# Recurrent attention and a gated feed-forward on one core: eps as a 385th column, PSUM rings named tile by tile, and another order of all steps

## The chip, the core and the metric

The kernel runs on one core of a Trainium2 chip. Five engines work side by side, each through its own list of instructions in a fixed order: TensorE (PE in the profile, with its weight loads as PEld), VectorE (DVE), ScalarE (ACT), GpSimd (POOL) and SyncE (SP), which here only issues transfers. The metric is the device time of one run in microseconds (us).

## What is computed

The reference first runs a recurrence over 768 tokens for 4 batches x 8 heads of width 48, and then a feed-forward over the 3072 tokens of width 384:

```python
# attention, for each token t; state is 48x48 per batch and head
y[t]  = r[t] @ (state + (u*k[t])^T v[t])
state = w[t][:, None] * state + k[t]^T v[t]
# feed-forward on x = y, heads side by side
xn  = x / sqrt(mean(x*x) + 1e-6) * rms_g
g   = xn @ w_gate
out = (g * sigmoid(g) * (xn @ w_val)) @ w_out
```

Inputs and output are float32; the kernel multiplies in bfloat16 and sums in float32.

## The kernel before

The tokens are cut into 6 blocks of 128 for each of the 4 batches. A step is named `step.n.j`: n is the block, j the batch (or, in the feed-forward, the unit of work x). Blocks 0 and 1 of a batch are loaded together and treated as a pair of 256 tokens.

For each block the attention part does the following. `load_w`, `load_r`, `load_k`, `load_v` bring the inputs in (SP). `ln` takes the log of w (ACT), `cs_mm` (and `cs_k`, `cs_add`) makes its prefix sums by matmul (PE, DVE), `exp_r` and `exp_k` turn them into factors (ACT), `r_mul` and `k_mul` scale r and k with them (DVE; most k_mul on POOL). `rk_pe` transposes the result on PE and `rk_tr` copies it out (in blocks 0 and 1), or `rk_tr` is a transposing transfer. `q_mm` makes the 128x128 score tiles (even heads and odd heads apart), `q_mask_e`, `q_copy_o` and `q_mask_o` mask them into the tile `qts`, `st_mm` and `st_new` carry the state, `y_mm` makes the attention's output in PSUM. `bonus_mul`, `bonus_sum` and `bonus_v` make the u term (POOL, DVE, POOL), whose u was spread over the partitions once by `gu_mm` and `gu_out`. `x_add` adds both into `xb` (DVE). `x_sq` squares it on ACT and sums the row, `x_rstd` makes the reciprocal root, `xn_mul` applies it. `xn_pe` with `xn_out`, or the transfer `xn_tr` with `xn_gain` on POOL (blocks 4 and 5), lays the tile out for the feed-forward as `xnt`.

The feed-forward of a block of 512 tokens has 12 units x. `gate_mm.n.x` and `val_mm.n.x` are 3 matmuls of 512 columns each (in block 0, 6 of 256), `silu` (ACT) empties the gate's PSUM bank into `sg`, `h_mul` (DVE) multiplies the value's bank with it into `ht`. `o_mm` is 12 matmuls of 384 columns, `o_out` copies its bank out, `out_dma` stores it. The weights come by `load_gv` and `load_wo`, issued by POOL: the first gates need `load_gv.1.0` (wg_sb), the first values `load_gv.1.1` (wv_sb). `warm` is a matmul of zeros; 13 stand at the start, the rest fill places where PE would wait.

Nothing is scheduled by the compiler: the table ORDER is a list of 1096 steps, and each engine's list is the order in which its instructions are met there. Small sets say which engine a step uses: CAST_ACT, XN_DVE, RK_DVE, ODD_DVE, RSTD_ACT, OUT_DVE. PSUM's 8 banks are in three rings: "a" (2 banks: gates and prefix sums), "b" (2: values and the k sums), "q" (4: all else). A step that needs a bank takes the longest unused one of its ring whose last user stands earlier in ORDER, and waits on the chip until that user is done.

ACT holds one table of functions at a time. `act()` loads "ln and exp" or "silu" when the step needs the other one than the last step did (L236); Copy and Square need no change. `x_rstd` is Ln and Exp on ACT where RSTD_ACT says so, otherwise on POOL two operations, scale and eps (L589) and a power (L590).

## Time and profile before

| | |
|---|---|
| median of 3 runs | 199.46 us (199.08 to 203.08) |
| span of the profiled execution, first to last instruction | 197.62 us |
| median of the runs less that span | 1.84 us |
| PE busy | 191.5 us of the span, 97% |
| DVE, ACT, POOL busy | 156.4, 139.1, 127.5 us |
| granted TensorE clock | 1.000 |
| table loads on ACT | 14, 1283 ns each |
| moved by transfers | 32.42 MB, mean 164 GB/s |

The profile does not give the profiled execution's own device time beside its span; the runs' median stands next to it in the table. "L646" in a row is line 646 of the kernel, `ps_au` the first bank of ring "a" (u, v, x, z number the banks), `A<-B` says that a tile A is made from B, and `<-PE ps_av` behind an idle time names what ended it. A group row has busy us and the mean ns of one, and then the idle time ahead of it. Matmuls overlap, so the distance from start to start is what one costs.

### The profile page before, as it was taken

What the parts mean: (1) busy time and instruction counts of PE and PEld (TensorE: products, weight loads), DVE (VectorE), ACT (ScalarE), POOL (GpSimd) and SP (SyncE); (2) the same over time, 40 slices, a digit from 0 to 9 for tenths busy, and PEclk for the clock granted to TensorE, in tenths of its full rate; (3) what the DMA queues carried; (4) which work ended last, traced back from release to release, by engine and by line L of the source; (5) the groups of instructions that cost most, each with busy time, mean ns of one, the idle gap of its engine ahead of it and who ended that gap; (6) DMA issues with size and microseconds to landing.
All of it is one profiled execution on the core that took longest, in us unless ns stands there. A gap on an engine that the chain in (4) does not pass through costs nothing.

```text
span 197.6 us, 4751 instructions
## 1 busy us (share of the span) xinstructions
PE 191.5 (97%) x1742; PEld 120.4 (61%) x1742; DVE 156.4 (79%) x315; ACT 139.1 (70%) x286; POOL 127.5 (64%) x181
## 2 busy tenths in 40 slices
PE   7899999999999999999999999999999999999994
PEld 3456677888665556655655655666655655555563
DVE  5699998999997999989799988997689842435530
ACT  3989998979997889795699875698556760514201
POOL 3399999988599759793969998599661544000000
PEclk9999999999999999999999999999999999999999
DMA  6999999999897999999999967924580021012112
GB/s 164 320 325 267 244 220 205 220 213 197 174 230 162 199 179 214 200 211 214 185 206 225 202 147 166 227 51 145 134 216 12 5 60 60 20 63 80 40 60 101
DMA packets 109807, 32.42 MB, mean 164 GB/s; under 512 B 104276, under 2 KB 108632, under 8 KB 109784
## 3 DMA queue, kind: packets, MB, share of 16 engines
q1 hardware_dynamic: 107744, 28.58, 63.4%
q0 software_dynamic: 2032, 3.54, 10.0%
q8 instruction: 13, 0.21, 0.5%
q14 instruction: 10, 0.08, 0.1%
q10 hardware_dynamic: 8, 0.00, 0.0%
HBM read 25.96 MB, written 4.72 MB: 155 GB/s over the span
## 4 chain that ended last, share of the span: by engine, by line
PE 83%; DMA 7%; POOL 6%; SPq 1%; issue 1%; ACT 0%; POOLq 0%
PE ps_bu L646 13%; PE ps_bv L646 12%; PE ps_av L646 11%; PE ps_au L646 11%; PE ps_qv L683 7%; PE ps_qx L683 6%; PE ps_qz L683 6%; DMA wv_sb<-in_moe_w_val_dram 5%; PE ps_qu L683 5%; DMA kt<-in_k_dram 2%; POOL ruk L464 1%; POOL ruk L465 1%; SPq L248 1%; POOL qts L536 1%; PE ps_qz L513 1%
## 5 line engine op out<-in xcount | busy, mean ns | idle before, releaser
L238 ACT ACTIVATE sg<-ps_av 128x512 bf16<-128x512 f32 x36 | 21.5, 596 | 27.1 <-PE ps_av L646 21.4
L683 PEld LDWEIGHTS <-ht 128*128 128x128 bf16 x312 | 28.6, 98 | 18.3 <-DVE ht L666 0.4
L646 PEld LDWEIGHTS <-wg_sb 128*128 128x128 bf16 x252 | 27.0, 114 | 16.6 <-issue 0.3
L646 PEld LDWEIGHTS <-wv_sb 128*128 128x128 bf16 x252 | 26.4, 114 | 16.0 <-DMA wv_sb<-in_moe_w_val_dram 0.7
L666 DVE TENSOR_TENSOR ht<-ps_bu,sg 128x512 bf16<-128x512 f32 x37 | 25.4, 687 | 10.7 <-PE ps_bu L646 8.3
L666 DVE TENSOR_TENSOR ht<-ps_bv,sg 128x512 bf16<-128x512 f32 x35 | 24.0, 686 | 9.9 <-PE ps_bv L646 8.5
L646 PE MATMUL ps_bu<-xnt,wv_sb 128*128 128x512 bf16 (+1 forms) x135 | 30.3, 343 | 0.5 <-DMA wv_sb<-in_moe_w_val_dram 0.5
L646 PE MATMUL ps_av<-xnt,wg_sb 128*128 128x512 bf16 (+1 forms) x126 | 29.4, 350 | 0.0
L646 PE MATMUL ps_au<-xnt,wg_sb 128*128 128x512 bf16 (+1 forms) x126 | 29.3, 349 | 0.1
L646 PE MATMUL ps_bv<-xnt,wv_sb 128*128 128x512 bf16 (+1 forms) x117 | 28.5, 358 | 0.0
L464 POOL TENSOR_TENSOR ruk<-rt,kt 128x384 f32<-128x384 f32 x24 | 24.0, 1002 | 1.9 <-DVE diag L469 1.4
L465 POOL TENSOR_TENSOR ruk<-ruk,u_bc 128x384 f32<-128x384 f32 x24 | 24.0, 1000 | 1.9
L238 ACT ACTIVATE sg<-ps_au 128x512 bf16<-128x512 f32 x36 | 21.5, 596 | 4.5 <-PE ps_au L646 3.3
L457 POOL TENSOR_TENSOR rk<-kt,ek 128x384 bf16<-128x384 f32 x20 | 19.8, 1001 | 6.6 <-DMA kt<-in_k_dram 5.5
L475 POOL TENSOR_TENSOR ydiag<-vt,diag 128x384 f32<-128x384 f32 x24 | 19.9, 836 | 1.0 <-DVE diag L469 1.0
L236 ACT ACT_TABLE_LOAD x14 | 18.0, 1283 | 1.9 <-PEq L729 1.6
L536 POOL TENSOR_SCALAR_AFFINE_SELECT qts<-qts 128x512 bf16<-128x512 bf16 x19 | 11.9, 637 | 11.2 <-ACT qts L533 8.0
L683 PE MATMUL ps_qv<-wo_sb,ht 128*128 128x384 bf16 (+1 forms) x96 | 15.5, 311 | 0.0
L581 ACT ACTIVATE junk<-xb 128x384 bf16<-128x384 f32 x24 | 12.5, 521 | 4.2 <-DVE xb L576 3.9
L469 DVE TENSOR_REDUCE diag<-ruk 128x8 f32<-128x384 f32 x24 | 13.0, 544 | 0.0
L683 PE MATMUL ps_qx<-wo_sb,ht 128*128 128x384 bf16 x72 | 12.7, 326 | 0.0
L683 PE MATMUL ps_qz<-wo_sb,ht 128*128 128x384 bf16 x72 | 12.7, 326 | 0.0
(212 smaller groups left out, 376.8 us busy)
## 6 DMA issues: line engine op xcount, KB each, us to landing
out_dram<-ob SPq DMA_DIRECT2D x19, 192.0 KB, 2.4
wt<-in_w_dram SPq DMA_DIRECT2D x16, 192.0 KB, 4.2
rt<-in_r_dram SPq DMA_DIRECT2D x16, 192.0 KB, 4.4
vt<-in_v_dram SPq DMA_DIRECT2D x16, 192.0 KB, 3.7
kt<-in_k_dram SPq DMA_DIRECT2D x16, 192.0 KB, 4.0
wt<-in_w_dram SPq DMA_DIRECT2D x4, 384.0 KB, 4.3
rt<-in_r_dram SPq DMA_DIRECT2D x4, 384.0 KB, 4.9
kt<-in_k_dram SPq DMA_DIRECT2D x4, 384.0 KB, 4.9
```

Of the source, the lines that this page charges most:

```text
L236: nc.scalar.preload_act_table_set(table_name)
L238: return nc.scalar.activation(**kw).ins
L457: eng.tensor_tensor(out=rk[:, n % 2, j, 1, :, 0:D], in0=inp["k", n, j], in1=bank["cs_k", n, j][:, 0:DM].rearrange("p (h d) -> p h d", h=H) ...
L464: eng.tensor_tensor(out=ruk[n, j], in0=inp["r", n, j], in1=inp["k", n, j], op=ALU.mult)
L465: eng.tensor_tensor(out=ruk[n, j], in0=ruk[n, j], in1=u_bc, op=ALU.mult)
L469: nc.vector.tensor_reduce(out=diag[n, j].rearrange("p h o -> p (h o)"), in_=ruk[n, j], axis=mybir.AxisListType.X, op=ALU.add)
L475: eng.tensor_tensor(out=ydiag[n, j], in0=inp["v", n, j], in1=diag[n, j].to_broadcast([128, H, D]), op=ALU.mult)
L536: nc.gpsimd.affine_select(out=qts[n, j][:, 1], in_=qts[n, j][:, 1], compare_op=ALU.is_ge if n < 2 and j // 4 < n else ALU.is_gt, fill=0.0, ...
L581: nc.scalar.activation(out=junk, in_=xb[n, j], func=AF.Square, accum_out=rstd[n, j][:, 0:1])
L646: nc.tensor.matmul(ps.rearrange("p (i t) -> p i t", t=cols.stop - cols.start)[:, i, :], lhsT=units(ws, c, fs.start + i), rhs=xnt[n][:, c, ...
L666: nc.vector.tensor_tensor(out=ht[n][:, fs, cols], in0=bank.pop(("v", n, f)).rearrange("p (i t) -> p i t", i=fs.stop - fs.start), in1=bank. ...
L683: nc.tensor.matmul(ps[:, cols], lhsT=ht[n][:, f, b * L:(b + 1) * L], rhs=wo_sb[:, f, cols], start=(f == 0), stop=(f == FC - 1))
```

## The change

Three things, in one diff.

1. The sum of squares is finished on ACT. `xb` is no longer a rotating tile of 384 columns but one of 4 rows of `xrow`, with a 385th column that holds the square root of 384 eps. The Square has scale 384^-0.5 and runs over 385 columns, so its row sum is mean(x*x) + eps. On POOL only the power is left, and on ACT the Ln has no scale and no bias. The multiplication by rms_g in blocks 4 and 5 was on POOL and stays there; the unused other branch goes.
2. Tables MOVED_Q, MOVED_A and MOVED_B name a ring for 231 PSUM tiles; `psum()` looks there first. Gates and values may now lie in "q", scores, states and outputs in "a" or "b".
3. All of ORDER is new (1090 steps: 32 warm for 34, 15 q_mask_o for 19, else the same steps), and so are the sets. By the two programs: table loads 14 to 20; xn products on DVE 6 to 13; o_out on DVE 11 to 7; rk_tr copies on DVE 4 to 2; score tiles masked on DVE 45 to 49, copied by ACT 19 to 15; casts of v on ACT 13 to 14; Ln and Exp pairs on ACT 8 to 6; POOL's scale-and-eps operations 16 to none and its powers 16 to 18. SP issues the same 136 transfers.

```diff
-    CAST_ACT = sel("00 01 02 03 10 13 20 21 31 32 41 52 53")
+    CAST_ACT = sel("00 01 02 10 11 12 23 30 31 33 41 42 50 51")
-    XN_DVE = sel("02 21 23 42 43 51")
+    XN_DVE = sel("03 12 13 21 30 32 33 40 41 42 43 50 51")
-    RK_DVE = sel("00 11 12 13")
-    ODD_DVE = sel("00 01 02 04 12 13 15 16 20 21 43 50 53")
-    RSTD_ACT = sel("00 10 11 21 22 23 41 42")
-    OUT_DVE = sel("02 11 22 23 30 33 41 42 50 52 53 54")
+    RK_DVE = sel("00 02")
+    ODD_DVE = sel("04 06 07 10 11 12 13 15 16 22 23 32 40 42 43 50 52")
+    RSTD_ACT = sel("10 20 23 32 33 42")
+    OUT_DVE = sel("02 03 23 31 41 43 55")
...
     def psum(ring, key, shape, dtype=FP32):
+        ring = moved.get(key, ring)
         slots = rings[ring]
...
+    xrow = const.tile([128, NXB, DM + 16], FP32)
+    nc.vector.memset(xrow[:, :, DM:DM + 1], (eps * DM) ** 0.5)
...
     def x_add(n, j):
-        xb[n, j] = pt.tile([128, DM], FP32, name="xb", bufs=NXB)
-        nc.vector.tensor_tensor(out=xb[n, j], in0=bank.pop(("y", n, j)),
+        k = min((x for x in range(NXB) if xslots[x][0] < at[0]), key=lambda x: xslots[x])
+        xslots[k] = [xlast[n, j], NXB + at[0]]
+        xb[n, j] = xrow[:, k, 0:DM + 1]
+        nc.vector.tensor_tensor(out=xb[n, j][:, 0:DM], in0=bank.pop(("y", n, j)),
                                 in1=ydiag[n, j].rearrange("p h d -> p (h d)"), op=ALU.add)
     def x_sq(n, j):
-        nc.scalar.activation(out=junk, in_=xb[n, j], func=AF.Square, accum_out=rstd[n, j][:, 0:1])
+        nc.scalar.activation(out=junk[:, 0:DM + 1], in_=xb[n, j], func=AF.Square, scale=DM ** -0.5,
+                             accum_out=rstd[n, j][:, 0:1])
     def x_rstd(n, j):
-            act(LN_EXP, out=ss, in_=ss, func=AF.Ln, scale=1.0 / DM, bias=eps_col)
+            act(LN_EXP, out=ss, in_=ss, func=AF.Ln)
...
-            nc.gpsimd.tensor_scalar(out=ss, in0=ss, scalar1=1.0 / DM, scalar2=eps, op0=ALU.mult, op1=ALU.add)
             nc.gpsimd.tensor_tensor(out=rstd[n, j][:, 1:2], in0=ss, in1=mhalf, op=ALU.pow)
```

What the new order does is seen in the engines' lists, at the places that the prediction speaks of. First POOL, from the load of the first gate weights (wg_sb, `load_gv.1.0`) to that of the first value weights (wv_sb, `load_gv.1.1`); ydiag is bonus_v, the affine select q_mask_o, rk a k_mul, vb a cast of v; the numbers tell tiles of one name apart. Before:

```order
L350 DMA wg_sb4_138<-in_moe_w_gate_dram 128x3x1024
L475 TENSOR_TENSOR ydiag_346<-vt_278,diag_283 128x384
L536 AFFINE_SELECT qts_314<-qts_314 128x512
L536 AFFINE_SELECT qts_363<-qts_363 128x512
L475 TENSOR_TENSOR ydiag_440<-vt_278,diag_402 128x384
L536 AFFINE_SELECT qts_474<-qts_474 128x512
L384 CAST vb_500<-vt_348 128x384
L350 DMA wv_sb4_140<-in_moe_w_val_dram 128x3x1024
```

And now:

```order
L357 DMA wg_sb4_136<-in_moe_w_gate_dram 128x3x1024
L550 AFFINE_SELECT qts_285<-qts_285 128x512
L489 TENSOR_TENSOR ydiag_385<-vt_381,diag_383 128x384
L550 AFFINE_SELECT qts_326<-qts_326 128x512
L471 TENSOR_TENSOR rk_129<-kt_460,ek_416 128x8x48
L489 TENSOR_TENSOR ydiag_478<-vt_381,diag_308 128x384
L550 AFFINE_SELECT qts_474<-qts_474 128x512
L606 TENSOR_TENSOR rstd_513<-rstd_513,mhalf_126 128x1
L357 DMA wv_sb4_138<-in_moe_w_val_dram 128x3x1024
```

A k_mul and the power of the first block have come in between, and a cast has left.

Second DVE, up to its first h_mul (`ht`), which is the first reader of a value unit. Before, the score masks (`qts` with `up`) among its last rows are three:

```order
L451 TENSOR_TENSOR rk_131<-rt_400,ps_bv_423 128x8x48
L457 TENSOR_TENSOR rk_131<-kt_404,ps_qu_627 128x8x48
L576 TENSOR_TENSOR xb_728<-ps_qz_709,ydiag_704 128x384
L523 TENSOR_TENSOR qts_699<-ps_qx_689,up_117 128x512
L528 TENSOR_TENSOR qts_699<-ps_qv_690,up_117 128x512
L523 TENSOR_TENSOR qts_754<-ps_qu_744,up_117 128x512
L489 COPY rkT_775<-ps_qx_766 128x1024
L619 TENSOR_TENSOR xnt_633<-ps_qv_784,gT_77 128x3x128
L666 TENSOR_TENSOR ht_789<-ps_bu_777,sg_680 128x2x256
```

Now seven stand there, those of the q_mm that moved ahead of the first value unit on PE among them:

```order
L465 TENSOR_TENSOR rk_129<-rt_548,ps_qv_556 128x8x48
L537 TENSOR_TENSOR qts_672<-ps_qx_662,up_117 128x512
L537 TENSOR_TENSOR qts_749<-ps_qz_739,up_117 128x512
L542 TENSOR_TENSOR qts_760<-ps_au_751,up_117 128x512
L537 TENSOR_TENSOR qts_760<-ps_qu_750,up_117 128x512
L542 TENSOR_TENSOR qts_795<-ps_bv_786,up_117 128x512
L537 TENSOR_TENSOR qts_795<-ps_qz_785,up_117 128x512
L537 TENSOR_TENSOR qts_821<-ps_bu_811,up_117 128x512
L635 TENSOR_TENSOR xnt_591<-ps_bv_842,gT_77 128x3x128
L635 TENSOR_TENSOR xnt_591<-ps_qz_857,gT_77 128x3x128
L678 TENSOR_TENSOR ht_892<-ps_au_825,sg_720 128x2x256
```

The first value unit lies in a bank of ring "a" now (ps_au, before ps_bu), and more score tiles are masked ahead of it.

Third ACT in the feed-forward of block 3 (`sg` is a silu, `lw` an ln of a later block, `ob` an o_out, `vb` a cast). Before:

```order
L238 ACTIVATE ek<-ps_bv 128x384
L238 ACTIVATE lw<-wt 128x8x48 x2
L236 ACT_TABLE_LOAD
L238 ACTIVATE sg<-ps_av 128x512
L238 ACTIVATE sg<-ps_au 128x512
L692 COPY ob<-ps_qv 128x384
L238 ACTIVATE sg<-ps_av 128x512
```

Now:

```order
L247 ACTIVATE sg<-ps_qz 128x512
L394 CAST vb<-vt 128x384 x2
L245 ACT_TABLE_LOAD
L247 ACTIVATE lw<-wt 128x8x48
L245 ACT_TABLE_LOAD
L247 ACTIVATE sg<-ps_qx 128x512
L245 ACT_TABLE_LOAD
L247 ACTIVATE lw<-wt 128x8x48
L704 COPY ob<-ps_qz 128x384
L245 ACT_TABLE_LOAD
L247 ACTIVATE sg<-ps_qu 128x512
```

Two ln that stood together ahead of the silu units stand alone between them, with a table load on each side.

235 lines of the change are left out of this document (121 added, 114 removed).

## The prediction

> **What bounds the kernel now.** I read the busy shares first, then the table by stages, then TensorE (PE) in order of time, then who waits for whom.
>
> ```profile
> PE 191.5 (97%) x1742; PEld 120.4 (61%) x1742; DVE 156.4 (79%) x315; ACT 139.1 (70%) x286; POOL 127.5 (64%) x181
> ```
>
> The table by stages, with busy us (instructions) of PE, weight loads, DVE, ACT and POOL, then the granted clock:
>
> ```profile
> 0.00:10.80 10.80, 8.86 (x62) 5.00 (x63) 6.95 (x29) 6.26 (x10) 4.38 (x15) 1.00 0.91 249
> 10.80:25.80 15.00, 14.29 (x209) 8.86 (x207) 15.00 (x33) 14.87 (x33) 14.71 (x19) 1.00 1.16 276
> 25.80:30.80 5.00, 4.51 (x65) 3.74 (x65) 5.00 (x10) 4.95 (x10) 4.75 (x7) 1.00 1.11 209
> 30.80:75.00 44.20, 44.20 (x474) 32.17 (x475) 41.56 (x80) 38.71 (x75) 36.15 (x49) 1.00 1.01 197
> 75.00:130.00 55.00, 54.98 (x475) 32.61 (x474) 49.77 (x99) 43.44 (x96) 44.39 (x62) 1.00 0.94 196
> 130.00:160.00 30.00, 30.00 (x255) 17.92 (x253) 25.07 (x48) 20.90 (x48) 19.40 (x29) 1.00 0.34 92
> 160.00:194.70 34.70, 34.70 (x212) 20.12 (x209) 13.09 (x22) 9.78 (x18) 3.67 (x6) 1.00 0.18 57
> ```
>
> From 30.8 to 194.7 us PE is busy without a gap at clock 1.00. A busy PE need not be at its peak, so two neighbouring groups of that stretch, in order of time (start, length), show the pace:
>
> ```profile
> 167.24 0.81 PE L646 MATMUL ps_av<-xnt,wg_sb 128*128 128x512 bf16 x3
> 167.89 0.81 PE L646 MATMUL ps_au<-xnt,wg_sb 128*128 128x512 bf16 x3
> ```
>
> A gate or value unit starts 0.65 us after the one before it, here and wherever two stand together. So behind 30.8 us the time is a sum of fixed PE work: an order can lose there, and gain only what PE does earlier. Ahead of 30.8 us PE waits, or runs zero matmuls as filler, because DVE, ACT and POOL are full from 10.8 us on (15.00, 14.87 and 14.71 of 15.00). The front ends with a transfer:
>
> ```profile
> 25.79 0.82 PE L646 MATMUL ps_au<-xnt,wg_sb 128*128 128x256 bf16 x6
> 30.79 0.84 PE L646 MATMUL ps_bu<-xnt,wv_sb 128*128 128x256 bf16 x6 [0.49 <-DMA wv_sb<-in_moe_w_val_dram]
> ```
>
> The chain of waits has the same transfer, issued by POOL:
>
> ```profile
> 20.98 9.76 DMA wv_sb<-in_moe_w_val_dram
> ```
>
> The sum is made on this execution's span of 197.62 us; the median of the runs, 199.46, lies 1.84 above, and I carry the 1.84 over unchanged.
>
> **Term 1: PE work moved ahead of the first value unit.** Comparing the two step lists up to the first val_mm, the new one has every PE step of the old one there, and five more: st_mm.0.1, rk_pe.0.3, q_mm.0.2, q_mm.0.6, q_mm.1.7. Their prices are distances between starts:
>
> ```profile
> 22.51 0.50 PE L545 MATMUL ps_qu<-vb,rk 128*128 128x96 bf16 x8
> 22.85 0.56 PE L562 MATMUL ps_qx<-vb,qts 128*128 128x48 bf16 x16
> 23.30 0.61 PE L482 MATMUL ps_qv<-ident,rk 128*128 128x128 bf16 x8
> 23.74 0.33 PE L612 MATMUL ps_qz<-ident,xn 128*128 128x128 bf16 x3
> ...
> 26.44 0.82 PE L646 MATMUL ps_av<-xnt,wg_sb 128*128 128x256 bf16 x6
> 27.19 0.23 PE L501 MATMUL ps_qx<-rkT 48*128 48x128 bf16 x1
> ...
> 27.52 0.57 PE L562 MATMUL ps_qz<-vb,qts 128*128 128x48 bf16 x16
> ```
>
> st_mm costs 22.85 - 22.51 = 0.34, rk_pe 0.44, a q_mm 0.33 and some 0.07 of the gap of 0.10 ahead of it (26.44 + 0.65 = 27.09), so 0.40. Sum: 0.34 + 0.44 + 3 x 0.40 = 1.98 us less work behind that point. No filler stands behind it in either kernel; the two fillers fewer (32 for 34) are inside the front and count nothing of their own.
>
> **Term 2: when the first value unit starts.** Two things must be there. First the transfer. Ahead of its issue POOL gets a k_mul (L457, 1.00 us), a pow (L590, 0.57) and one mask instead of another, and loses a cast (L384):
>
> ```profile
> 8.18 1.00 POOL L457 TENSOR_TENSOR rk<-kt,ek 128x384 bf16<-128x384 f32 x1 [5.53 <-DMA kt<-in_k_dram]
> ...
> 20.54 0.49 POOL L384 CAST vb<-vt 128x384 bf16<-128x384 f32 x1
> ...
> 26.59 0.57 POOL L590 TENSOR_TENSOR rstd<-rstd,mhalf 128x1 f32<-128x1 f32 x1
> ```
>
> That is 1.08 later (1.00 + 0.57 - 0.49). Against it, POOL's chain starts earlier: the k load, for which it waited 5.53 us, moves from fourth to third in SP's queue, one place or 1.2 us (SP's queue, start and length):
>
> ```profile
> 3.23 1.15 SPq L248 DMA_DIRECT2D kt<-in_k_dram  x1
> 4.42 1.15 SPq L248 DMA_DIRECT2D rt<-in_r_dram  x1
> ```
>
> But gu_mm, which ran behind the first prefix sum, now runs ahead of it on PE:
>
> ```profile
> 6.59 0.91 PE L367 MATMUL ps_qx<-u_bc,ones_row 1*128 1x384 f32 x2
> 7.34 0.28 PE L369 MATMUL ps_qz<-i,g_row 3*128 3x3 f32 x2
> 7.54 0.50 PE L397 MATMUL ps_av<-lw,mid 128*128 128x384 bf16 x2
> ```
>
> It takes 0.95 us there (7.54 - 6.59), and the exp that k_mul needs is behind it. So I take 0.5 of the 1.2 us: issue at 20.98 + 1.08 - 0.5 = 21.6. The pow also waits for ACT's square of the first block:
>
> ```profile
> 20.09 0.59 ACT L581 ACTIVATE junk<-xb 128x384 bf16<-128x384 f32 x1
> ```
>
> Ahead of that square ACT has 25 steps' work now and 26 before, so it comes about as late, and the issue is 21.6 to 22.2. I take 21.9, and with the old 9.76 us the weights land at 31.7. Second, PE's own way: the old first gate came at 25.79, and the lists ahead of it got no longer (DVE gets five instructions of its usual kinds and loses seven, ACT gets five and loses six), so 25.8 again at the latest. Behind it, ahead of the first value unit, stand 4 gates (0.65), 5 q_mm (0.40), 2 rk_pe (0.44) and a y_mm (23.30 - 22.85 = 0.45): 5.9 us, so 31.7 too, an agreement that leaves no cover on either side. That is 0.9 later than 30.79. Bounds: 31.0, if the gate comes 0.7 earlier (one DVE instruction) and the transfer with it; 33.8, if POOL waits for ACT 2.1 us, its longest such wait (below).
>
> **What is moved or swapped at no cost.** POOL loses 16 scale-and-eps operations and 4 masks, 16 x 0.189 + 4 x 0.637 = 5.6 us, and is 64% busy: no gain but in the chain of one block. ACT gains 6 table loads and loses 7 xn products; DVE gets those:
>
> ```profile
> L236 ACT ACT_TABLE_LOAD x14 | 18.0, 1283 | 1.9 <-PEq L729 1.6
> L597 ACT ACTIVATE xn<-xb,rstd 128x384 bf16<-128x384 f32 x18 | 11.0, 610 | 0.7 <-POOL rstd L590 0.6
> L238 ACT ACTIVATE lw<-wt 128x384 bf16<-128x384 f32 x16 | 8.1, 518 | 0.0
> L589 POOL TENSOR_SCALAR rstd<-rstd 128x1 f32<-128x1 f32 x16 | 3.0, 189 | 8.9 <-ACT junk L581 8.2
> L536 POOL TENSOR_SCALAR_AFFINE_SELECT qts<-qts 128x512 bf16<-128x512 bf16 x19 | 11.9, 637 | 11.2 <-ACT qts L533 8.0
> ```
>
> 6 x 1.28 - 7 x 0.61 = +3.4 us on ACT. The cover is ACT's idle time, 11.6 of 55 us between 75 and 130, and most of its waits are for PE:
>
> ```profile
> ACT sg L238 <- PE ps_av L646: 21.4, 16, 6.0
> POOL rstd L589 <- ACT junk L581: 8.2, 8, 2.1
> ```
>
> Without that cover it is the slower rival. PSUM rings: each tile now names its ring, so a gate may use any of 8 banks instead of 2; no copy is added. The 385th column adds one element to a 521 ns square. At block 5, PE goes from its last y_mm to the first gate over one value unit and four o_mm (0.65 + 4 x 1.95 = 8.45 us). The old chain there:
>
> ```profile
> 156.64 0.36 PE L571 MATMUL ps_qx<-vb,qts 128*128 128x48 bf16 x8
> ...
> 163.10 2.39 POOL L625 TENSOR_TENSOR xnt<-xnt,gT 128x384 bf16<-128x384 bf16 x3 [1.65 <-DMA xnt<-xn]
> ```
>
> 157.0 to 165.5 is 8.5 us, less some 0.3 for the operation and the handover that the pow no longer has ahead of it: 0 expected, up to 2 if a queue holds it. The tail is alike: last o_mm of 96 columns, one copy, one store.
>
> **Sum.** 197.62 - 1.98 + 0.9 = 196.5; with 1.84, 198.4 us. With the bounds of term 2, 197.7 to 200.5.
>
> **Rivals.** *The front gives nothing back:* the weights land at 32.8 or later, since POOL waits for ACT ahead of the issue; or block 5 waits. Term 1 is eaten: 199.5 to 201.5. For it: POOL is full until then, and ACT too. Against: the queues ahead of the issue grew by only 1 us.
>
> *Slower:* table switches. In the new order ACT has places where one ln stands alone between two silu: 1.28 + 0.52 + 1.28 = 3.1 us in which no gate leaves PSUM. PE can ask for a bank again 1.3 us later (two units). A fully exposed pair costs 1.8 us; the six more loads make three such pairs, 5.4 us: 203.8. It decides from about three fully exposed pairs on. Against: the wider rings and ACT's idle time. On the price of a switch, the old rows:
>
> ```profile
> 25.99 1.28 ACT L236 ACT_TABLE_LOAD   x1
> 27.28 0.60 ACT L238 ACTIVATE sg<-ps_au 128x512 bf16<-128x512 f32 x1
> ```
>
> The next operation starts 1.29 us after the load's start. The Trainium skill (ScalarE: Activation LUTs, What ACT_TABLE_LOAD costs) adds a drain of about 1.38 us to each load, 2.66 us a switch; by that the pair would be 5.8 us, and three exposed pairs an estimated 13.6 us, near 212 us. The trace shows no such drain here, so that case gets 1 in 100, inside the slower rival.
>
> *Much faster:* the front shrinks too, the first value unit at 28.7 instead of 31.7: 195.4. Against: the three engines that feed it are full from 10.8 us on with the same work.
>
> **How the numbers follow.** The forecast (197.4 to 199.2) gets 0.50, the eaten gain 0.30, slower than 203.4 by table switches 0.13, the faster front 0.07. The range 196.4 to 202.5 leaves those last two out, 0.20. Two per cent of 199.46 is 4.0 us, about what a measurement of this kernel can tell from no change: faster than 195.5 gets 0.07, within 0.80, slower 0.13.
>
> **What would show it.** Term 1 and 2: the first value unit near 31.7 after a wait for wv_sb, PE without a gap from there, and its last matmul near 193.6. The eaten gain: that unit at 32.8 or later, or a gap of PE ahead of block 5's first gate. Slower: PE waiting for ACT's silu around table loads. I am wrong if PE has gaps of over 1 us in all behind the first value unit.

## The result and the profile after

The changed kernel takes 207.81 us (median of 4 runs, 206.77 to 208.69), the kernel before beside it 199.37: a ratio of 1.0412, 95% interval 1.0369 to 1.0456. It is slower by 4%, some 8.4 us; the forecast was 198.4 us, in a range that ended at 202.5. Here and below the medians are of all runs, while the ratios leave out every run that lies over 1.5% above the fastest of its kernel.

The profiled execution of the changed kernel has a span of 206.0 us and an own time of 207.69. First the busy shares, then the table by stages, as for the kernel before, with the stretch from 75 to 130 us cut in two:

```profile
PE 195.1 (95%) x1725; PEld 122.5 (59%) x1740; DVE 158.8 (77%) x319; ACT 145.3 (71%) x285; POOL 123.3 (60%) x162
```

```profile
0.00:10.80 10.80, 9.75 (x44) 4.95 (x45) 5.65 (x27) 4.88 (x7) 3.15 (x14) 1.00 0.92 250
10.80:25.80 15.00, 13.90 (x177) 8.25 (x175) 12.68 (x25) 12.96 (x25) 12.89 (x16) 1.00 1.16 294
25.80:30.80 5.00, 4.76 (x81) 3.61 (x80) 5.00 (x13) 4.95 (x12) 4.65 (x6) 1.00 1.11 192
30.80:75.00 44.20, 43.88 (x498) 33.67 (x498) 42.22 (x82) 39.12 (x74) 38.10 (x50) 1.00 0.96 185
75.00:95.00 20.00, 16.49 (x147) 9.80 (x148) 16.24 (x36) 15.51 (x37) 14.80 (x17) 1.00 1.07 213
95.00:130.00 35.00, 33.87 (x292) 19.91 (x295) 30.89 (x60) 29.71 (x57) 22.99 (x28) 1.00 0.91 190
130.00:160.00 30.00, 29.84 (x228) 17.63 (x226) 25.27 (x48) 20.18 (x42) 19.16 (x24) 1.00 0.42 109
160.00:203.00 43.00, 42.60 (x286) 24.66 (x287) 20.85 (x36) 17.70 (x37) 7.60 (x11) 1.00 0.14 41
```

Two things differ from the table of before. From 10.8 to 25.8 us DVE, ACT and POOL were full; now each idles for over 2 us. And from 75 to 95 us PE idles 3.51 us, where before it had no gap. Behind the first value unit PE loses 0.32 + 3.51 + 1.13 + 0.16 + 0.40 = 5.52 us in all (length less busy, row by row). The first value unit itself comes 4.50 us later than before (35.29 for 30.79):

```profile
29.55 0.71 PE L658 MATMUL ps_av<-xnt,wg_sb 128*128 128x256 bf16 x5
...
35.29 0.85 PE L658 MATMUL ps_au<-xnt,wv_sb 128*128 128x256 bf16 x6
```

With the prediction's own sum, 197.62 - 1.98 + 4.50 + 5.52 = 205.66, against the 206.0 measured: the two losses account for this execution's span to 0.3 us. PE does not wait for wv_sb ahead of its first value unit here. Its first gate comes at 29.55, and from there it works for 5.74 us, without a wait of note, until the value unit.

**The front.** TensorE in its first microseconds, in the changed kernel:

```profile
5.33 1.64 PE L379 MATMUL ps_qv<-u_bc,ones_row 1*128 1x384 f32 x2
...
8.59 0.85 PE L433 MATMUL ps_av<-lw,mid 128*128 128x384 bf16 x2
9.23 0.85 PE L433 MATMUL ps_qz<-lw,mid 128*128 128x384 bf16 x2
...
12.64 0.86 PE L496 MATMUL ps_au<-ident,rk 128*128 128x128 bf16 x8
13.34 0.61 PE L496 MATMUL ps_qv<-ident,rk 128*128 128x128 bf16 x8
```

A pair of matmuls of 384 columns lasts 0.85 us here, where the pair in the prediction's row at 7.54 lasted 0.50; one starts 9.23 - 8.59 = 0.64 us behind the other, while single zero matmuls of that width, once the pace has doubled in experiment 1, stand 0.16 apart. So the array runs at half pace until about 13 us (a transpose group lasts 0.86 at 12.64 and 0.61 at 13.34), while the column of the granted clock shows 1.00. In the profile of before the pace had doubled by 5.3 us. The prefix sums and the first transposes come later by that, and what needs them with them.

**The body.** PE's gaps of 0.7 us or more behind 36 us:

```profile
90.23 0.81 PE L658 MATMUL ps_qz<-xnt,wg_sb 128*128 128x512 bf16 x3 [1.11 <-ACT ob L704]
...
93.39 0.23 PE L527 MATMUL ps_bv<-rkT 48*128 48x128 bf16 x1 [2.02 <-DMA rkT<-rk]
...
116.72 0.34 PE L628 MATMUL ps_au<-ident,xn 128*128 128x128 bf16 x3 [0.73 <-DVE xn L611]
```

The first is `gate_mm.2.2`, whose bank in the new rings is one that an o_out has to empty. ACT comes to that copy late, because it waits with the copy ahead of it for a store to free an output buffer:

```profile
89.09 0.48 ACT L704 COPY ob<-ps_bv 128x384 f32<-128x384 f32 x1 [1.41 <-DMA out_dram<-ob]
89.70 0.48 ACT L704 COPY ob<-ps_qz 128x384 f32<-128x384 f32 x1
```

The second gap is inside `q_mm.3.0`: its first half has run at 90.97, and its second half waits for the transposing transfer `rk_tr.3.1`. The store and the transpose both stand in SP's queue. SP's queue after (start, length):

```profile
83.97 0.92 SPq L267 DMA_DIRECT2D rt<-in_r_dram  x1
...
85.82 1.06 SPq L719 DMA_DIRECT2D out_dram<-ob  x2
86.98 1.32 SPq L501 DMA_TRANSPOSE rkT<-rk  x1
88.35 0.57 SPq L267 DMA_DIRECT2D kt<-in_k_dram  x1
88.97 2.38 SPq L501 DMA_TRANSPOSE rkT<-rk  x1
```

and before:

```profile
81.53 1.75 SPq L487 DMA_TRANSPOSE rkT<-rk  x1
83.72 0.36 SPq L707 DMA_DIRECT2D out_dram<-ob  x1
84.27 4.01 SPq L487 DMA_TRANSPOSE rkT<-rk  x3
```

SP issues one transfer after the other here, nearly without a pause, in both kernels. By the two step lists, nine loads of blocks 4 and 5 stand ahead of block 3's second `rk_tr` now, four before. The transposes are issued at 86.98 and 88.97, before at 81.53 and 84.27, some 5 us later. PE asks for them earlier in its work than in the old order: six units of the feed-forward that stood ahead of `q_mm.3.0` stand behind it now, one has come ahead, and five units are some 3.3 us at 0.65.

### The profile page after: what moved, and what is told of

Read it like the earlier page. It is cut to its first block, busy times and chain, and to the rows that moved or that the text cites. A ratio compares the mean times of both kernels' runs of the same rounds, so it can differ in the third digit from the quotient of the medians.

```text
span 206.0 us, 4685 instructions
## 1 busy us (share of the span) xinstructions
PE 195.1 (95%) x1725; PEld 122.5 (59%) x1740; DVE 158.8 (77%) x319; ACT 145.3 (71%) x285; POOL 123.3 (60%) x162
## 4 chain that ended last, share of the span: by engine, by line
PE 67%; ACT 14%; DVE 8%; DMA 4%; issue 3%; POOL 2%; SPq 1%; DVEq 0%; ACTq 0%
PE ps_qu L658 6%; PE ps_av L658 5%; PE ps_bu L658 5%; PE ps_qv L658 5%; PE ps_qx L658 4%; PE ps_au L658 4%; PE ps_qz L658 4%; ACT L245 3%; PE ps_av L695 3%; ACT junk L597 3%; PE ps_qv L695 3%; PE ps_bv L695 3%; PE ps_bv L658 3%; ACT sg L247 3%; DMA rt<-in_r_dram 2%
## 5 line engine op out<-in xcount | busy, mean ns | idle before, releaser
L606 POOL TENSOR_TENSOR rstd<-rstd,mhalf 128x1 f32<-128x1 f32 x18 | 10.0, 572 | 13.1 <-ACT junk L597 13.0
L597 ACT ACTIVATE junk<-xrow 128x385 bf16<-128x385 f32 x24 | 12.6, 526 | 1.3 <-DVE xrow L592 1.0
L695 PE MATMUL ps_qv<-wo_sb,ht 128*128 128x384 bf16 x72 | 12.7, 326 | 0.0
L247 ACT ACTIVATE lw<-wt 128x384 bf16<-128x384 f32 (+1 forms) x20 | 11.3, 583 | 1.8 <-DMA wt<-in_w_dram 1.7
L678 DVE TENSOR_TENSOR ht<-ps_qu,sg 128x512 bf16<-128x512 f32 x14 | 9.6, 687 | 2.6 <-PE ps_qu L658 1.4
L658 PE MATMUL ps_qu<-xnt,wv_sb 128*128 128x512 bf16 (+1 forms) x47 | 11.3, 352 | 0.1
L658 PE MATMUL ps_qz<-xnt,wg_sb 128*128 128x512 bf16 (+1 forms) x35 | 8.9, 361 | 1.2 <-ACT ob L704 1.1
L247 ACT ACTIVATE sg<-ps_qz 128x512 bf16<-128x512 f32 x11 | 6.6, 599 | 4.1 <-DVE ht L678 3.9
L678 DVE TENSOR_TENSOR ht<-ps_bu,sg 128x512 bf16<-128x512 f32 x11 | 7.5, 684 | 2.4 <-ACT sg L247 1.9
L247 ACT ACTIVATE sg<-ps_au 128x512 bf16<-128x512 f32 x10 | 6.0, 596 | 4.5 <-PE ps_au L658 2.4
```

Of the source, the lines that this page charges most:

```text
L247: return nc.scalar.activation(**kw).ins
L597: nc.scalar.activation(out=junk[:, 0:DM + 1], in_=xb[n, j], func=AF.Square, scale=DM ** -0.5, accum_out=rstd[n, j][:, 0:1])
L606: nc.gpsimd.tensor_tensor(out=rstd[n, j][:, 1:2], in0=ss, in1=mhalf, op=ALU.pow)
L658: nc.tensor.matmul(ps.rearrange("p (i t) -> p i t", t=cols.stop - cols.start)[:, i, :], lhsT=units(ws, c, fs.start + i), rhs=xnt[n][:, c, ...
L678: nc.vector.tensor_tensor(out=ht[n][:, fs, cols], in0=bank.pop(("v", n, f)).rearrange("p (i t) -> p i t", i=fs.stop - fs.start), in1=bank. ...
L695: nc.tensor.matmul(ps[:, cols], lhsT=ht[n][:, f, b * L:(b + 1) * L], rhs=wo_sb[:, f, cols], start=(f == 0), stop=(f == FC - 1))
```

## The experiments

Ratios are against the kernel before, run beside each kernel, with their 95% interval. A diff of ORDER shows moved steps only; dots stand for the steps between.

### 1 and 2. The front: gu_mm behind the prefix sums, and ahead of them in the old kernel

```diff
 a1_gu_late, against the changed kernel
-warm.212.0 gu_mm.0.0 load_w.0.0 ... exp_k.1.0 gu_out.0.0 ... cs_mm.0.1 w_tot.0.0
+warm.212.0 load_w.0.0 ... exp_k.1.0 ... cs_mm.0.1 gu_mm.0.0 gu_out.0.0 w_tot.0.0
 b1_gu_first, against the kernel before
-warm.212.0 ... exp_k.0.0 gu_mm.0.0
+warm.212.0 gu_mm.0.0 ... exp_k.0.0
```

> The changed kernel with one step moved back: the u and g matmuls (f32, one and three rows of the array) run behind the second prefix sum on TensorE instead of ahead of the first. Clock theory: in the changed kernel every matmul from 5.3 to 13.4 us runs at half the pace (the two 128x384 of a prefix sum 0.64 us apart, 0.33 in the kernel before), because these two matmuls keep the array nearly empty just when its clock would have been raised; moved back, the pace doubles between 5 and 8 us, the first value unit comes about 3 us earlier than 35.3, and the time is 204 to 205.5 for 207.8. Order theory (the two matmuls only take their own 0.95 us on TensorE and the half pace has another cause): the half pace stays until about 13 us and the time is 206.8 to 207.8.

> The kernel before with one step moved forward: the same two f32 matmuls run ahead of its first prefix sum, as in the changed kernel; nothing else is touched. Clock theory: half pace until 10 to 14 us, the first value unit 2 to 3.5 us later than 30.8, time 201.5 to 203. Order theory: only the 0.95 us of the two matmuls lie ahead of the first prefix sum, the time is 199.5 to 200.4.

a1: 208.2 us, ratio 1.0397 [1.0334, 1.0460]. In its profile the pace doubles at about 4.2 us, and the first value unit comes at 32.14:

```profile
3.91 0.46 PE L389 MATMUL ps_qv<-zero 128*128 128x384 bf16 x1
4.21 0.33 PE L389 MATMUL ps_qx<-zero 128*128 128x384 bf16 x1
4.37 0.33 PE L389 MATMUL ps_qz<-zero 128*128 128x384 bf16 x1
```

This profiled execution is 2.2 us shorter than that of the changed kernel (span 203.8 for 206.0), but the median is not better: its five other runs have spans of 205.8 to 207.1 with a mean granted clock of 0.983 to 0.992, and the changed kernel's other three 205.0 to 207.0 at 0.983 to 0.992. Nor does all of the earlier start reach the end: the first value unit is 3.15 us earlier, the span 2.2. Experiment 5 shows one fall of the clock.

b1: 200.1 us, ratio 1.0030 [0.9998, 1.0061]. The profiled execution doubled its pace only at about 10 us and has a span of 199.4, 1.8 above that of before; apart from one run of 201.8 at clock 0.992, its spans fall into 197.4 to 198.1 and 198.6 to 199.8.

So gu_mm first does not always make the front late. Two kernels below (a2, a3) have it first too, doubled their pace by 4.2 us and reached the first value unit at 32.1 and 31.5. All twenty profiles, one execution each, sort by where gu_mm stands. In the fourteen kernels that have it behind the first prefix sum, the pace doubles between 3.9 and 6.9 us. In the six that have it first, the pace has doubled by 4.2 us, before gu_mm starts (a2, a3), or it doubles only between 10 and 13 us (the changed kernel, b1, a4 and d2). So gu_mm, with 1 and 3 rows in use, postpones the doubling where it has not come by the time gu_mm starts, 5.3 us in these four.

The Trainium skill (TensorE: Matmul & The Clock Gate, What's actually happening) has the array start at half rate, released after one busy window of about 3.4 us that runs freely and does not start with the kernel. The 3.9 to 6.9 us of the fourteen agree with a window whose phase is chance; 10 to 13 us need more than the phase. That nearly empty matmuls count as idle in it is my reading; the sorting fits it, and no run here isolates it.

### 3. The 385th column alone

```diff
 b3_eps, against the kernel before: xrow, the scaled Square over 385 columns, one power; old order, rings and sets
-        nc.scalar.activation(out=junk, in_=xb[n, j], func=AF.Square, accum_out=rstd[n, j][:, 0:1])
+        nc.scalar.activation(out=junk[:, 0:DM + 1], in_=xb[n, j], func=AF.Square, scale=DM ** -0.5,
+                             accum_out=rstd[n, j][:, 0:1])
...
-            nc.gpsimd.tensor_scalar(out=ss, in0=ss, scalar1=1.0 / DM, scalar2=eps, op0=ALU.mult, op1=ALU.add)
```

> The kernel before with the 385th column alone: eps goes into the square's sum, the reciprocal root is one pow on GpSimd or Ln and Exp on ScalarE, 16 short GpSimd operations go; order, rings and engines as before. The prediction's term for it is 0: 199.0 to 200.0. A cost of its own (the 385 column square, the shared row buffer) would show as 201 or more; a gain as 198.5 or less.

199.58 us, ratio 0.9990 [0.9956, 1.0025]. The column and the missing POOL operation are worth nothing that can be told, as the prediction had it. The loss lies in order, rings and sets.

### 4. Table loads between silu, in the kernel before

```diff
 b2_tables, against the kernel before: three pairs of loads that nothing needs
+        if (n, f) in ((1, 6), (2, 4), (3, 8)):
+            nc.scalar.preload_act_table_set(LN_EXP)
+            nc.scalar.preload_act_table_set(SILU)
```

> The kernel before with six table loads more and nothing else: at three places in the middle of a run of silu steps (one in each of blocks 1, 2 and 3) ScalarE loads the other table and the silu table again, 2.57 us each time. The prediction's no-cost term: ScalarE's idle time covers them, 199.4 to 200.4. The prediction's slower rival: 1.8 us for each exposed pair, 5.4 in all, 204.8; by the Trainium skill's drain on top of each load more still, about 212.

205.39 us, ratio 1.0274 [1.0210, 1.0337]. One of the pairs on ACT, and PE behind it, in the trace of b2:

```profile
66.36 1.28 ACT L661 ACT_TABLE_LOAD   x1
67.65 1.28 ACT L662 ACT_TABLE_LOAD   x1
68.95 0.60 ACT L238 ACTIVATE sg<-ps_au 128x512 bf16<-128x512 f32 x1
```

```profile
70.32 0.81 PE L646 MATMUL ps_bu<-xnt,wv_sb 128*128 128x512 bf16 x3 [0.90 <-DVE ht L669]
```

PE falls 2.1, 0.6 and 1.7 us behind its list at the three pairs, some 4.5 us, 1.5 for each on average (the first, shown above, stands right ahead of a pair that the old list has already): the price that the prediction's slower rival gave an exposed pair was 1.8. So the price is real. But the changed kernel does not pay it where the prediction looked. Its ln that stand alone between silu, and PE there:

```profile
124.08 1.28 ACT L245 ACT_TABLE_LOAD   x1
125.38 0.53 ACT L247 ACTIVATE lw<-wt 128x384 bf16<-128x384 f32 x1
125.92 1.28 ACT L245 ACT_TABLE_LOAD   x1
127.22 0.60 ACT L247 ACTIVATE sg<-ps_qx 128x512 bf16<-128x512 f32 x1
```

```profile
120.00:132.00 12.00, 11.95 (x102) 6.87 (x102) 9.70 (x18) 10.86 (x16) 7.64 (x11) 1.00 0.78 172
```

PE is busy 11.95 of the 12 us around them: the wider rings let it go on. The new kernel has that cover at this place.

### 5. The xn products of block 3 on ACT

```diff
 a3_xn, against the changed kernel
-    XN_DVE = sel("03 12 13 21 30 32 33 40 41 42 43 50 51")
+    XN_DVE = sel("03 12 13 21 40 41 42 43 50 51")
```

> The changed kernel with three normalising products of block 3 (parts 0, 2, 3) back on ScalarE instead of VectorE. In the changed kernel they stand in a row on VectorE at 114 to 116.6 us and take 1.03, 0.41 and 1.15 us, where the same product takes 0.41 while GpSimd is idle; TensorE waits 0.9 us at 115.8 for the last. Contention theory: the 0.9 us gap goes, 206.5 to 207.2 for 207.8. Chain theory (the product waits for its reciprocal root and the queue, the engine makes no difference): no change, 207.5 to 208.2.

207.20 us, ratio 1.0363 [1.0313, 1.0412]: no gain that can be told. Ahead of block 3's gates PE now waits 0.95 and 0.16 us for ACT, where it waited 0.73 for DVE. But DVE's products in the changed kernel are worth a look. DVE and POOL there:

```profile
77.30 0.41 DVE L611 TENSOR_SCALAR xn<-xrow,rstd 128x384 bf16<-128x384 f32 x1
...
114.16 1.03 DVE L611 TENSOR_SCALAR xn<-xrow,rstd 128x384 bf16<-128x384 f32 x1
115.19 1.48 DVE L611 TENSOR_SCALAR xn<-xrow,rstd 128x384 bf16<-128x384 f32 x2
```

```profile
113.98 1.00 POOL L471 TENSOR_TENSOR rk<-kt,ek 128x384 bf16<-128x384 f32 x1
115.24 1.21 POOL L471 TENSOR_TENSOR rk<-kt,ek 128x384 bf16<-128x384 f32 x1 [0.26 <-ACT ek L247]
```

A product takes 0.41 us while POOL is idle, and 1.03 when a k_mul of POOL is under way: it ends 0.21 us behind the end of the k_mul (114.98, then 115.19), and so does the last of the pair (116.45, 116.67). The Trainium skill (SBUF — State Buffer, Who interferes with whom) has a port pair that DVE, in some operations, shares with GpSimd as an exclusive lock, the later one blocked until the other is done. The rows agree with it; the loss that a3 could have won back is about 0.7 us, below what its interval can tell.

The profile of a3 shows what the gaps do to the clock. TensorE, then the granted clock behind the busy times:

```profile
88.00:92.40 4.40, 1.56 (x20) 0.77 (x20) 1.97 (x4) 3.45 (x6) 4.32 (x5) 1.00 1.12 200
92.40:95.80 3.40, 3.40 (x9) 1.22 (x10) 1.88 (x3) 2.27 (x4) 1.36 (x3) 0.53 1.03 203
```

Behind 4.4 us in which PE was busy for 1.56, the clock is 0.53 for 3.4 us. A unit costs 1.28 us there (93.36 to 94.64 in the timeline) and not 0.65, so such a fall takes about 1.7 us on top of the gaps. The mean clock of 0.983 to 0.992 in the other runs of the changed kernel, of a1 and of a3 is what one such fall of 3.4 us in 206 gives (0.47 x 3.4 / 206 = 0.008), or two. The Trainium skill (TensorE: Matmul & The Clock Gate, HAM oscillation — how this bites in real kernels) lets the clock fall after a single idle gap of over 3.4 us; here the two gaps were 1.18 and 2.03 us, so shorter ones close together can be enough. They are not always: the profile of the changed kernel has gaps of 1.11 and 2.02 us at the same steps, that of a1 1.32 and 2.01, PE is busy for only 1.27 and 1.17 of 4.4 us around them, and the clock stays at 1.00 in both.

### 6 and 7. SP's queue: block 3's transposes earlier, and four small transfers ahead of them in the old kernel

```diff
 a2_sp_order, against the changed kernel
-load_v.3.2 o_mm.1.3 load_w.5.2 ... load_r.4.2 ... load_v.3.0 ... out_dma.0.2 ... out_dma.0.3 ... rk_tr.3.0 ... load_k.4.3 ... rk_tr.3.1
+load_v.3.2 rk_tr.3.1 out_dma.0.2 rk_tr.3.0 out_dma.0.3 load_v.3.0 o_mm.1.3 load_w.5.2 ... load_r.4.2 ... load_k.4.3
 c2_loads, against the kernel before: four loads of 16 columns of r into a tile that nothing reads
-silu.1.11
+silu.1.11 load_x.5.0 load_x.5.1 load_x.5.2 load_x.5.3
+    def load_x(n, j):
+        nc.sync.dma_start(out=spare[:, j], in_=r[j, :, n * L:(n + 1) * L, 0:D // 3].rearrange("h t d -> t h d"))
```

> The changed kernel with SP's queue put in another order at one place: the transposing transfers of block 3's first two parts and the two stores of block 0 go ahead of three loads that are needed only later. Queue theory: TensorE's two gaps at 88.7 and 91.2 us (1.3 and 2.2 us) come from those transfers being issued at 86.97 and 88.96 behind loads for blocks 4 and 5; with the new order the transfers are issued some 4 us earlier and 2.5 to 3.5 us of the two gaps go: 204.3 to 205.3 for 207.8. Table theory (ScalarE's table loads between 70 and 77 us make the products late, and the transfers with them): the transfers are issued earlier but wait for their products, less than 1 us is gained: 206.8 or more.

> The kernel before with four small transfers more on SP's queue (1024 pieces of 64 bytes each, to a place that nobody reads), at about 66 us, ahead of what block 3 waits for; the changed kernel has five more loads there than the kernel before. Queue theory: block 3's transposing transfers come 3 to 4 us later, TensorE gets gaps where it had none, 1.5 to 4 us in all: 201 to 203.5. Rival (SP has time to spare there and the loss in the changed kernel has another cause): 199.2 to 200.2.

a2: 205.99 us, ratio 1.0314 [1.0266, 1.0362], some 1.8 us better than the changed kernel in the median and between the two theories. The transposes go out at 80.00 and 83.08, and PE waits for neither of them. It waits 0.87 at `gate_mm.2.2` and, in place of the wait for the transpose, 0.55 for a silu; then 1.03 for the next transpose (at 95.16) and 0.62 for a silu (at 103.56). PE's idle time behind the first value unit is 5.05 us in all, for 5.5 in the changed kernel, and the span of 203.9 is no shorter than that of a1's one execution at clock 1.00 with as early a front (203.8). So the gaps have mostly moved. What differs more is the clock: 0.999 or 1.00 in all six runs, where three of the changed kernel's four read 0.983 to 0.992.

c2: 203.60 us, ratio 1.0194 [1.0156, 1.0232]. SP in c2:

```profile
70.36 3.19 SPq L264 DMA_DIRECT2D spare<-in_r_dram  x4
...
86.83 1.82 SPq L493 DMA_TRANSPOSE rkT<-rk  x1
```

Four transfers more take SP 3.2 us, and the transposes of block 3 go out 5.2 us later than in the kernel before (86.83 for 81.53): SP's queue around 70 to 90 us is full in the old kernel already. But PE waits for none of the transposes. Its two new gaps are elsewhere in c2:

```profile
84.70 0.34 PE L618 MATMUL ps_qx<-ident,xn 128*128 128x128 bf16 x3 [0.67 <-ACT xn L603]
...
86.36 2.11 PE L689 MATMUL ps_qz<-wo_sb,ht 128*128 128x384 bf16 x12 [0.89 <-DVE ob L696]
```

The second waits for an o_out on DVE that itself waited 1.03 us for a store. Across these two gaps PE falls 1.9 us behind the kernel before. Another 2.2 us of the 4.4 by which this span is longer were lost ahead of the first value unit (32.95 for 30.79), where DVE waited 3.1 us for a late k load, as it did in the profiles of b2 and b3, which have the old front too. So c2 is slower by 1.9%, and a full queue of SP does cost the old kernel time, by way of a store and not of the transposes; how much of the 1.9% is the queue's, one trace does not show.

### 8 to 10. Repairs together

```diff
 a4_loads, against a2_sp_order
-load_k.3.3 load_v.3.1 silu.1.1 load_r.5.2 ... load_k.3.1 ... load_v.4.1 ... load_k.3.2 ... load_r.3.3 ... load_r.3.2 ... load_v.3.2 rk_tr.3.1 ...
+load_k.3.3 load_k.3.1 load_r.3.3 load_r.3.2 load_k.3.2 load_v.3.1 load_v.3.2 load_v.3.0 silu.1.1 ... rk_tr.3.1 out_dma.0.2 rk_tr.3.0 out_dma.0.3 load_r.5.2 load_v.4.1 ...
 a5_all: a1_gu_late, a3_xn and a4_loads together
 a6_store, against a5_all
-out_dma.0.0 ... q_copy_o.4.1 out_dma.0.1
+out_dma.0.0 out_dma.0.1 ... q_copy_o.4.1
```

> The changed kernel with SP's queue in another order from the first store on: the k, r and v loads of block 3 stand ahead of the loads of blocks 4 and 5 again, and its two first transposing transfers and two stores ahead of four of those loads. Queue theory, widened: in the changed kernel six loads of later blocks push the last r and k loads of block 3 from 74 to 82 us; GpSimd waits for them (4.4 us for r, 2.9 for k in one run) and hands its products on late; with the new order TensorE's gaps between 77 and 95 us shrink from some 5 to under 2 us, time 203.5 to 205. Table theory: ScalarE is the late one, the gaps stay above 3.5 us and the time is 206 or more.

> The three repairs together on the changed kernel: u and g matmuls behind the prefix sums, SP's queue with block 3 first, three products of block 3 on ScalarE. If the losses are the slow array clock at the start (about 2 us), SP's queue (about 4) and the three products (about 1), the time is 200 to 202, within 1 per cent of the kernel before. If table loads or the ring names carry most of the loss, it is 204 or more.

> The kernel with the three repairs and one store moved: the second store of block 0, which the changed kernel issues only behind the first gates of block 3, goes next to the first. Buffer theory: until then it holds one of the three output buffers from 57 to 120 us, so the copy of a block 1 product waits for another store, and a gate, whose ring now names that product's bank, waits for the copy (1.2 us at 87.1); that gap goes, 0.7 to 1.3 us less than the three repairs alone. Rival: the gap only moves to the next wait behind it, no change within 0.5 us.

a4: 207.07 us, 1.0305 [1.0243, 1.0366]; in its profile gaps of 1.24, 0.55, 1.34, 0.53 and 0.73 us remain, and its front is as late as the changed kernel's (first value unit at 35.29). a5: 205.54 us, 1.0270 [1.0227, 1.0314], the best in the new order; all its runs have a clock of 0.998 to 1.00. In its profile PE waits 1.62 for a transpose at 97.03, 0.82 for an o_out, 0.95 for xn. a6 frees the output buffer early, which `out_dma.0.1` held from 57 to 120 us: the wait at `gate_mm.2.2` goes, but the store is one more transfer ahead of the transposes, and the last two of block 3 go out at 91.90 and 94.40, in a5 at 91.20 and 93.37. PE waits in a6:

```profile
95.61 0.23 PE L527 MATMUL ps_au<-rkT 48*128 48x128 bf16 x1 [2.27 <-DMA rkT<-rk]
98.21 0.28 PE L527 MATMUL ps_qu<-rkT 48*128 48x128 bf16 x1 [2.20 <-DMA rkT<-rk]
```

208.71 us, 1.0465 [1.0425, 1.0504]: slower, and both theories of it fall. The one place in SP's queue was dearer than the wait that it removed; and the clock is 0.983 to 0.992 in all six runs, where a5 kept 0.998 or more.

### 11 and 12. The scores of block 3 later

```diff
 a7_qlate, against a5_all (a tile takes another ring where its own has no free bank)
-out_dma.0.3 load_r.5.2 load_v.4.1 load_w.5.2 ... cast_v.3.0 q_mm.3.0 ... val_mm.2.4 rk_tr.3.2 ... h_mul.2.7 rk_tr.3.3
+out_dma.0.3 ... r_mul.3.3 rk_tr.3.2 rk_tr.3.3 load_r.4.2 load_k.4.3 load_v.4.1 load_w.5.2 load_r.5.2 ... h_mul.2.7 q_mm.3.0
 a8_both: a7_qlate and the store of a6_store
```

> The kernel with the three repairs, and block 3's score matmuls put later in TensorE's work: the changed kernel asks for them after 81.8 and 87.1 us of TensorE work, the kernel before after 85.4 and 88.8; here they stand behind six and one more units, and the two later transposing transfers stand ahead of five loads that nothing waits for yet. Cover theory: the loss of block 3 is TensorE asking for the scores some 4 us earlier in its work than their inputs can be there; 1.5 to 3 us less than the three repairs alone, about 203. Rival (ScalarE or GpSimd has less than it can do in that stretch, so the wait only moves to the scores' users): less than 0.7 us.

> Both of these on top of the three repairs: 201.5 to 203 if the gaps add up, 204 or more if the wait only moves on.

a7: 208.42 us, 1.0423 [1.0383, 1.0463]. a8: 209.91 us, 1.0518 [1.0482, 1.0554]. PE no longer waits for a transpose but for a mask on POOL. PE and POOL in a8:

```profile
101.33 0.46 PE L586 MATMUL ps_bu<-vb,qts 128*128 128x48 bf16 x7 [5.04 <-POOL qts L551]
```

```profile
98.62 0.99 POOL L479 TENSOR_TENSOR ruk<-rt,kt 128x384 f32<-128x384 f32 x1 [7.56 <-DMA rt<-in_r_dram]
...
100.64 1.22 POOL L551 TENSOR_SCALAR_AFFINE_SELECT qts<-qts 128x512 bf16<-128x512 bf16 x2
```

POOL stands 7.56 us at a bonus product of block 4 whose r load now comes late in SP's queue, and the mask of block 3 is queued behind it. The delay went from SP's queue to POOL's.

### 13. Zero matmuls in the gap

```diff
 a9_fill, against a1_gu_late
-cast_v.3.0 q_mm.3.0
+cast_v.3.0 warm.310.1 ... warm.321.1 q_mm.3.0
```

> The changed kernel with the u and g matmuls late, and twelve zero matmuls (1.9 us) put into TensorE's wait ahead of block 3's first scores; they compute nothing and the wait is longer than they are. Gap theory: two gaps of 1.3 and 2.2 us within 5 us make the array's clock fall to half pace for 3.4 us behind them in most executions (granted clock 0.98 to 0.99 in five of six, span 205.8 to 207.1 where the one at clock 1.00 took 203.8); with the gap filled the clock stays at 1.00 and the span at 203.5 to 204.5, time 205.2 to 206.2 for 208.2. Rival: the clock falls for another reason, or the fillers cost their 1.9 us: 208 or more.

210.36 us, 1.0413 [1.0369, 1.0456]. Four of six runs keep clock 1.00, at spans of 205.0 to 205.7 in three and 208.9 in one; two fall to 0.984 and 0.992 (211.6 and 210.3). In its trace the fillers do stand in the gap, which shrinks from 2.01 to 0.3 us; the span is 1.8 us longer than a1's at clock 1.00, but 1.5 of that is there before the first filler. As a repair it fails. More of its runs keep the clock than of a1's (four of six for one), but on the split between gap and clock it is inconclusive.

### 14 to 16. All of block 3 first on SP, with what hangs on it

```diff
 c3_queues, against a5_all: every load of block 3 and its four rk_tr ahead of blocks 4 and 5 on SP, but for two w loads
-load_v.3.1 load_v.3.2 ... load_w.4.3 ... load_w.4.2 ... load_r.5.2 load_v.4.1 load_w.5.2 ... cast_v.3.2 bonus_mul.4.3
+load_v.3.1 load_v.3.0 load_w.4.0 load_v.3.3 load_v.3.2 ... r_mul.3.3 rk_tr.3.2 rk_tr.3.3 load_r.4.3 load_k.4.3 load_w.4.3 load_w.4.2 ... bonus_v.3.2 bonus_mul.4.3
 c1_queues_q: c3_queues and the later q_mm of a7_qlate
 c4_exp, against c3_queues: part 3.1 in the table stretch of the ln ahead
-ln.3.0 ... val_mm.1.11 cs_mm.3.1 ... exp_r.3.1 ... exp_k.3.1 k_mul.3.1
+ln.3.0 cs_mm.3.1 cs_add.3.1 exp_r.3.1 w_tot.3.1 exp_k.3.1 k_mul.3.1 r_mul.3.1 ... val_mm.1.11
```

> The kernel with the three repairs and the queues put right all the way down: on SP every load, transposing transfer and store that block 3 waits for stands ahead of the loads of blocks 4 and 5, and on GpSimd the first bonus product of block 4, which waits for one of those loads, stands behind block 3's masks. Queue theory: each earlier repair only handed the wait to the next instruction behind a late load (the scores, then GpSimd's masks behind block 4's bonus product, then a cast of v); with all of them out of the way TensorE loses under 2 us between 77 and 110 us, where the three repairs alone lose 5: 201.5 to 203.5. Rival (SP and the transfer engines are full in that stretch, whatever the order): 205 or more.

> The same with block 3's score matmuls later in TensorE's work as well. If the masks behind block 4's bonus product were what cost the run with late scores its gain, this is 1 to 3 us faster than it (208.4), and 0 to 1.5 us faster than the kernel with the queues put right alone.

> The kernel with the queues put right, and the two exponentials of block 3's part 1 (with the prefix sum ahead of them) taken out of the third table stretch into the first, ahead of the silu steps between: the same number of table loads, but GpSimd's first product of block 3 can start some 3 us earlier. Table theory (the lone logarithms between silu steps make block 3 late): 1 to 2.5 us faster than with the queues put right alone. Queue theory: within 0.7 us of it.

c3: 208.87 us, 1.0413 [1.0362, 1.0464]; c1: 209.49 us, 1.0506 [1.0470, 1.0542]; c4: 210.41 us, 1.0521 [1.0483, 1.0559]. In c3's profile, of the longest of its six runs (210.24 us), PE's gaps between 77 and 110 us are 0.4 to 0.7 us each, and one of 4.15 us comes at 117.21. PE and ACT there:

```profile
117.21 0.34 PE L628 MATMUL ps_qx<-ident,xn 128*128 128x128 bf16 x3 [4.15 <-ACT xn L613]
```

```profile
116.17 0.48 ACT L704 COPY ob<-ps_av 128x384 f32<-128x384 f32 x1 [3.08 <-DMA out_dram<-ob]
116.54 1.12 ACT L613 ACTIVATE xn<-xrow,rstd 128x384 bf16<-128x384 f32 x2
```

The loads of blocks 4 and 5 that SP had put off now stand ahead of a store, ACT's copy waits 3.08 us for that store, and the xn products wait behind the copy. The times that the queue theory gave these kernels were not met. c4 tests whether the three table loads between 70 and 78 us, with exp_k.3.1 behind them, start the loss: in the changed kernel's profile POOL had waited 2.25 us for that exponential, up to 78.86. Taking that part out of there gained nothing (210.41 for 208.87), so the theory falls for this order of SP's queue; with the changed kernel's own queue it was not tried.

### 17 and 18. Sets without order, and order without sets

```diff
 d1_sets, against the kernel before, with b3_eps: the changed kernel's CAST_ACT, XN_DVE, RK_DVE, RSTD_ACT, OUT_DVE
+    CAST_ACT = sel("00 01 02 10 11 12 23 30 31 33 41 42 50 51")
...
 d2_sets_back, against the changed kernel: CAST_ACT, XN_DVE, RK_DVE, OUT_DVE of before
+    CAST_ACT = sel("00 01 02 03 10 13 20 21 31 32 41 52 53")
...
```

> The kernel before with the 385th column and with the changed kernel's choice of engine for the casts, the normalising products, the transposed copies, the reciprocal roots and the output copies; its own order and rings (the score copies stay as its order needs them). Order theory: what costs the 8 us is the order of the steps, the engine choices alone give 199 to 201. Engine theory (13 products on VectorE for 6, 7 output copies for 12, other casts): 203 or more.

> The changed kernel with the choice of engine of the kernel before for the casts, the normalising products, the transposed copies and the output copies; order, rings, column and reciprocal roots as changed. Order theory: 206 to 209, as the changed kernel. Engine theory: 203 or less.

d1: 221.34 us, 1.1082 [1.1036, 1.1128]. d2: 216.78 us, 1.0802 [1.0740, 1.0865]. New sets in the old order cost 22 us, old sets in the new order some 8 more than the new ones (1.0802 for 1.0412). d1 meets the engine theory's 203 or more, d2 the times of neither theory: neither order nor sets alone carry the loss, and neither half can be priced by taking it alone.

No version beat both kernels; b3 at 0.9990 is the kernel before within its interval.

## Why the prediction was wrong

- **What bounds the kernel** was right as far as it went: behind 30.8 us an order can lose there. The prediction said so and then put no price on losing. That is the first step that failed, and 5.52 us are what it left out.
- **Term 1, 1.98 us:** about right. From the first value unit to PE's last matmul it is 163.9 us before (30.79 to 194.70, 0.02 of it idle) and 167.7 now (35.29 to 202.98, 5.5 idle), so 1.7 us less work. The work is less, as forecast; the losses cover it.
- **Term 2, 0.9 us later:** it was 4.50, and this is the second step that failed. Of its two conditions the transfer was reckoned well: where the pace doubles early, wv_sb is issued at 21.64 (a3), 22.17 (a1) and 22.19 (a2), within the forecast 21.6 to 22.2, and the first value unit comes at 31.5, 32.1 and 32.1, for 31.7. Yet PE waits for that transfer in none of them; its own way sets the time. What failed is "25.8 again at the latest" for the first gate: it came at 29.55, and the 5.74 us from there are as forecast (5.9). The prediction priced gu_mm's move at 0.95 us of full-pace time; the half pace until 13 us it lacked. The profile of before could not show that, since there the half pace ended by 5.3 us.
- **"What is moved or swapped at no cost":** this is where the other loss lies, 5.52 us of PE idle behind the first value unit. The prediction counted POOL's queue ahead of wv_sb and ACT's tables, but never SP's queue, in which block 3's transposes moved behind five more loads. The profile of before would have warned of it: SP issues nearly without a pause from 62 to 92 us, and the share of DMA is 0.94 to 1.01 from 30.8 to 130. The two longest gaps, 1.11 and 2.02 us, end with a copy behind a store and with a transpose, both from that queue. What the move costs by itself is not shown: a2 takes the wait for the transpose away and has 0.5 us less idle time.
- **The clock** is in no term. Three of the changed kernel's four runs read 0.983 to 0.992, by a3's trace an estimated one or two falls of some 1.7 us each. The two kernels that kept 0.998 to 1.00 in every run, a2 and a5, have the best medians in the new order, though PE idles for 5.05 and 7.30 us behind the first value unit in their profiles.
- **The table loads:** no cost at 124 to 130 us, as forecast, and 1.5 us for a pair that is exposed (b2), near the rival's 1.8. The rival "slower" had the right sign, at 203.8 for 207.8, by a mechanism that neither this stretch nor c4 shows at work; that it came nearest is luck.
- **The 385th column at 0:** right (b3). **The hand-over to block 5 at 0:** PE's idle from 160 us on is 0.40 in all. **xn products on DVE:** one gap of 0.73 us, which is no smaller with ACT doing them.
- **"I am wrong if PE has gaps of over 1 us in all":** met, with 5.52, and this was the right place to look.

What stays open: no repaired order recovered the body's loss. In the traces of a6, a8 and c3 the wait that was aimed at is gone and another one on a different transfer or queue is there, and a7 and c1 were no faster; so the loss from 75 to 130 us looks like a chain through SP, ACT and POOL and not like one misplaced step, but its root is not isolated, and which arrangement would free all three was not found. Nor is the median of 207.81 split cleanly between late pace, gaps and the falls of the clock that follow the gaps, because the first and the last differ from run to run.

## What to carry to other kernels

Where one engine is busy without a gap, list every queue past which a reordering moves a step, the queue that only issues transfers among them, and price each late arrival before calling it free: SP has no row among the busy shares, and the two longest gaps here hang on transfers in its queue. A repair to one in-order queue puts something else late in it, so look for what now stands behind the moved transfers before expecting the gap's length back. And look at the spacing of the first matmuls, not at the clock column, to see at what pace a kernel starts.
